# Numerators and denominators by tokens for the first four head pairs of an attention-and-MLP kernel, in a new order

## The chip, the cores and the metric

One NeuronCore of one Trainium2 chip runs the whole program. The metric is the device time of one execution in microseconds (us); lower is better. The engines are TensorE (PE in the profile, with its weight loads as PEld), VectorE (DVE), ScalarE (ACT), GpSimd (POOL) and SyncE (SP), whose queue issues the DMAs. Each works through its own list of instructions in the order in which it was written, and waits on the others through semaphores.

## What is computed

Attention with random features, then a two-layer MLP with SiLU. For 8 batches of 8 heads, 576 tokens, head size 64 and 128 features:

```python
def phi(x):                                  # x: [tokens, 64] of one head
    proj = x @ omega.T                       # 128 features
    h = proj - sum(x * x) / 2
    return exp(h - max(h)) / sqrt(128)       # the maximum over the features
q_p, k_p = phi(q * scale), phi(k * scale)
kv  = k_p.T @ v                              # 128 x 64
z   = sum of k_p over the tokens             # 128
num = q_p @ kv                               # tokens x 64
den = q_p @ z + 1e-6                         # one number a token
attn = num / den
x = attn with the 8 heads side by side       # 4608 x 512
out = silu(x @ w_in) @ w_out                 # 512 -> 2048 -> 512
```

## The kernel before

Two heads make a **pair**; there are 32 pairs (n = 0 to 31), four of them a tile of tokens (one batch). Tile t of the MLP needs the pairs 4t to 4t+3. The MLP of the first three tiles is done plainly, in 16 steps f a tile (`stage1`, L886, three fp32r matmuls of 512 columns for each of the four pairs; then `silu`, `g_low`, and `stage2`, L1132). The rest goes through a scheme with fewer products (L971, L1085), which the change does not touch.

What a pair takes, with the engine of each step:

- `project` and `project_mid` (PE, L541, L547): features of 9 chunks of 128 tokens, tokens on the partitions. Chunk 4 holds 64 tokens of either head.
- `square` (ACT, L524), `square_sum` (DVE, L533), `top` (DVE, L554 and L556), `shift` (DVE, L562): the bias of the exponential.
- `expo` (ACT, L579): the features `hk` and `hq`, 128 tokens x 128 features a chunk.
- `zsum_direct` (PE, L628, L630): ten matmuls with a block of ones stationary and the features of k moving give z, repeated on all partitions.
- `kv` (PE, L651): ten matmuls with V stationary (64 columns wide, the two heads side by side) and the features moving. They give kv with V's columns on the partitions, so `kt_copy` (ACT, L656), `kv_turn` (PE, L659) and `kw_copy` (ACT, L664) turn it.
- `denom` (DVE, L639): ten fused multiply-and-sums of `hq` with z, each followed by a read of the accumulator, then a reciprocal (L644).
- `normal` (POOL, L669): three multiplications of `hq` by the reciprocal.
- `turn` (PE, L675) and `en_copy` (ACT, L685): the divided features with the features on the partitions.
- `numer` (PE, L711): four matmuls, kv stationary, features moving, in two rows of 512 and two of 64 columns; they give x with its columns on the partitions.
- `x_high` (ACT, L730), `x_low` (DVE, L735), `x_rest` (ACT, L740): x in two parts, as `stage1` wants it.

From pair 8 on z is summed on POOL, and from pair 5 on kv of the next pair and the numerator are one step; neither is changed.

The MLP's weights come as 64-bit words. For each block, ACT makes a scaled copy (`exponent`, L795), DVE builds the 32-bit number in three steps (`word`, L809, L811, L815), and POOL splits it (`weight_high` L828, `weight_low` L832).

The order on every engine is made when the program is built. A planner (`Plan.run`) takes one step after another by a due time (`key`), with costs (`COST`) and a table of shifts (`SHIFTS`, two characters a step) that moves each due time. PSUM has eight banks in four pools (`acc` 4, `h` 1, `fx` 1, `att` 2), given in turn. Where the planner sees PE idle it puts in filler matmuls on `ones` (`pulses`, L500), whose result nobody reads.

Of the kernel before, what the change touches and what calls it, by code (L numbers as in the profile page):

```python
# [42 lines left out]
LEAD = 4  # L43
WARM = 7
# [10 lines left out]
for _f in range(16):  # L55
# [3 lines left out]
HOMES |= {("raw", 3, "k"): "w12", ("raw", 3, "q"): "w13", ("v", 2): "w14", ("v", 3): "w15"}  # L59
PLAIN = 3  # L60
# [19 lines left out]
STAY = 5.387  # L80
HANDOFF = {"PE": 0.053, "ACT": 0.034, "DVE": 0.034, "POOL": 0.075, "SP": 0.08}
CALM = 0.341
JOIN = 0.929
WAIT_PE = 0.279
WAIT_ACT = 0.228
WAIT_DVE = 0.243
WAIT_POOL = 0.0
HASTE = 2.036
# [3 lines left out]
EASE = 0.082  # L92
# [11 lines left out]
    "nb": (0.29, 0.37), "ssum": (0.66, 0.745), "den": (3.41, 3.49),  # L104
# [10 lines left out]
    "AIAINlAIAIAIAIAIAIAIAIAqAIAIAPAIAIBXAIIhAIFMDPAIDrAIXZAOAIL0AIAIAIAIlUAIbNL-AIGTAILlYXAIAIAIZ1ALAIqbAICcCAJ1AI"  # L115
    "AIPLmFqsM6jGj+A6RmAIAkgMAIAiIvAIK7PnEpEkDhAJAIAISDAICbDJy9AIMlcGAIAIaLBJAIAIAmCToUFCDeAIAIAaAIAIFBNAc2AIvVAIv8"
    "cyD--4G8BnBqAIDyN9AIBjAbCjCeGwPwf5M2oxAIAIAI1YAIAIfvKUAIlAAIyJTCANqqE3CjT6AIAI-48PgXUTA3AIqVgEM7GqqoEaB3OHiXS7"
    "A0B6AOAIAde6AIMF9gTqNTAIBxMBSKAIAI5NAIAIfUhwSMAISBxVAIBqSpAIP7AIBal4tsAbOfAPAIrZv2nxm8AgAIAIS5JyJ+AIFeAJAIteLB"
    "O4E5R1EpENAICLAILNAIAIJfDhAIBwAIGPs4AIJrs7yrxrMlRPAIFIAgYaA3b9hRbmIIn9jzkT6LkovJsF29D+WOEC5KlVJbgh6nAIAkl6PAm6"
    "mkVzphES3T8Pha5xQn+L-UyFew72pi5OPWk0reil7VtnJIflaampwvp00rwVNdu0MlbFQ3mXIpFWXVQqTVWAh2n5lGMadWEFuMErPdltG3I-qz"  # L120
    "Njj8aLV-cUZEz92d39AIqdihAIAIfIA9w9AIA-+20PI88lPhg1dZAyrHN6CW-4JYJLhIAIm2YbHATZSbP1FlHzrMAIxbqCh6AeNPYGeEDRZFsK"
    "V260v0dWO17cdxwGIh6FFERZ7SVN8-6Y+ErCUPAIur-QGICPkQ3mTLqTgNn8yB455fx-u11n3A1DsOJatjjs09nPLXPmgj-4AIC2mdVWPZh82-"
    "xjzpvQAIvTynbmnYgSb8YhfaHoRB4R65pj6NcQmkjEKCYxVofLgLq1btU4iNXeYUbbXSJFJgWWTlLFaBSxmGFLebN1OuZIEtDlEoa0R6i-7i8X"
    "3hOpGSMDyZpXM2Tt2ybo2CJVdtsitDXRPPBkGPTrRwHVFvwHAIXXwOR4F3y+UOXAYYzBCySXA8JyWgRRRcG18vHmCFsmEaF6nJZphVkR6lzX-4"
    "NKBJG-eBVcLHUuEoOBldPSBWtZzb0g7eQKEPHZ6HLceiwdsoG-POE8yii5DsH3AIi4AIAIAIbuJqV+kQAuREAqDOOgAeLKbgknqhwCvE+IQzhg"
    "QOAwZFpr4WUm4Hg0aGD8FNti6bi6VFH2IGqIBHoaVEjfNNOh6+eqbJ1V0x+y-B8x0Tic5hQoMac2zg1AU7ODIYwaZWAIDXXm3hj6mvuUh6spNS"
    "pWcNUNLINoKMH2PyAIoB5TmFKvKzLZLQmZ6HVZ3oEekZAIVReEz17ryW6Mbok-b5LnPNrhg1YcRsjX0UeId1CSAIvxn4vpiAUDFvO0BFAIC+B0"
    "FrFbTvUEECApKUuSksWBUrCHlOJ0FR4dPNUzKgPYPHCfoc44rkr3rYtAP-4rXPDiOMMNLMMSaSAIMTgZEUAuFSNZL8UuSVPVG3AIBSWsE-fjVh"
    "BLA4B+UdAIr-+sR6EaYvI9vtY8APCsFFlNAIdWcsGVG-QnFjLDKYAMAIAISWU-F8kTZHJBCbAoBYZmAMAIASjIwU4xpv21AIAOkWdvQxIWC-r+"
    "mgHBGdytuN-3u2eyDdd5k1zrkcW-DD3qeEc0tElRgu4Gk1zWCyAINfAIs+dc0haFbJAeVF-4JQAI4FpQfP13979ut0A6RbRnZC1Vlye5qjFGf9"  # L130
    "AI8YzTcrjAAILGdf+6VRSKvcidj+knAIfq7erfv62f4uAsnO5ANEbyURoXRHOtRfUiq1BZGGmw9zei4+3L0hzY8diOuwwEcZiMmIB4Dq0ccHqj"
    "ss1b5wwcFV8dnUj2mooJCjAIbQYw42tdhH-4wU7MzYp1e5Z4xVwj6jdf7Wm1lA7l11dICcv7-4zT4D8ju2S3bPd+l7mDVTGqeoiNJq-45K3C7T"
    "FBAIElVBZG4FbZVFmongYIIr5w-48p5M-4-4yyx+AgJok5R47nL1-4AIsb-4efBt9-uV-4m48vvzXGBrNGjykkiQSkeImwQemccx6h-JIBAIDx"
    "BAsjRQPQzqA30by+Dvgrt9-4jsfBgCgUNKGUCow0nsRzn6iX5qO5c81AHeIRy-VPmd-4Cwl2qXuUQigIcVZQ3FabtQAIccGmAIAVqz-47rAITa"
    "bSyXyp3oiNLxWWLfeRp45c5O+L9AnBahluAjNPWhWj92TJ4OCbSElVAIDLYVLEQG4ec0eHnpgjJWD+AJJGZgWgSgF4RLWPD5ZTc1n9jqApAeAI"
    "S5HZAIFLFGFV1JBoWPridVw3w4iddKSCG0HGKQLjd8l6-etrFJ5HBuAI2AvQAIwCDdOEMSlsAIGusDD-KfAuHoE-IKzjJHUZXRLgEjAIGaE6He"
    "B+GuAOAIhqBHZ8bWbVl-ncsrsHk9BWKcmsAIUYqDF3EdYlSqGKAIObKQKvU3Hz8huAwNAIAvdxDfg0B9iHZ+zpk7T72f035xfBMt7iUKgzzSWa"
    "ZMA9G-Btu0734O4c8s8x3efhPGLLHoAIauBzmGFJtp3ohNAIo7c+gstbrhUjTZfTQEAIDoAncbA3T5AxBzGQZ8zbaHafNAJwnNAIaFm6uST0Td"
    "FMxeMLZcXKTFZLaE2fQPQtZAvWAIAIl0KoEEt1M5FOAIo5sLKtZDso1IhLfTAIAIOiOAIvatJpZzN7JletnCaGzBInAIZkcHDQY7k8UmVaWVXa"
    "B3EvAIAuCWFGBQAIAIQ5AIAIAIAIAIYiLFJ7AID4AISdMzdRzchYXaWBAIjAmWI4AIHCdSAIMjzYxxc1vgX+AIJoDbf3YE-4KeKGNCqBJgIZFn"  # L140
    "MoD8FbDUAIBdUclghSfZAIHBeYmxTvAIewdgEdHjlH+LqE9y1CCwfdz7dawYkYllPnmSj2ct-30evUcQbcgDJqBcBLxIYsC7jgtSo1wAmxyQp-"
    "nKdWh1dAMnrtbiZ9POaR4xqeL5rF1qYDxe1gIqlso-n-KgV3hzi+ryhMykJer4kn2M3w2YnzKY1HjnkttjgSBlsCYG4G0iucl+sundoMwLnOes"
# [48 lines left out]
)  # L191
HOT = 100.0
PULSE = 0.24
IDLE = 0.791
PAD = 0.288
EARLY = 0.9

# [80 lines left out]
class Plan:  # L278
# [20 lines left out]
    def cost(self, u):  # L299
# [15 lines left out]
        if kind == "sums":  # L315
            return ((0.79, 0.83), (0.79, 0.83), (0.79, 0.83), (0.45, 0.49), (0.45, 0.49))[n[2]]
        if kind == "wd" and n[-1] == 0:
            return 0.34, 0.42
# [145 lines left out]
def attention_mlp(ctx: ExitStack, tc: tile.TileContext, qT, kT, qn, kn, v, om_in, w_in, w_out, out, out_t):  # L464
# [53 lines left out]
    def load_v(n):  # L518
        T["v", n] = vt = new(HOMES.get(("v", n), "v"), [P, NC + 1, D])
        nc.sync.dma_start(vt, v[divmod(n, NPAIR)])  # L520
# [1210 lines left out]
```

## Time and profile before

| | us |
|---|---|
| median of 3 runs | 1010.08 (1009.83 to 1011.92) |
| the profiled execution | 1008.95 |
| span of its instructions | 1007.2 |
| PE busy in the span | 982.9 (98%) |
| DVE busy | 758.1 (75%) |
| ACT busy | 637.4 (63%) |
| POOL busy | 394.2 (39%) |
| mean granted TensorE clock | 0.995 |

A matmul on fp32 data shows as two records, each with its weight load; records overlap, so what a matmul takes on PE is the distance from one start to the next, not the length of a record. A wait in brackets stands on the instruction that waited, with the one that ended it.

### The profile page before, as it was taken

The numbers are of one execution on the slowest core, as the hardware profiler recorded it, in microseconds if no ns is written. First come the engines' busy times: TensorE is split into PE (matmuls) and PEld (weight loads), VectorE is DVE, ScalarE is ACT, GpSimd is POOL, SyncE is SP. The second block draws the span as 40 slices with busy tenths as digits, with TensorE's granted clock in tenths as the row PEclk, the third lists the DMA queues.
The fourth block names the chain that finished last, engine by engine and source line by source line (L and its number), as shares of the span: only waits on it lengthen the run. The fifth ranks groups of instructions, "written<-read, shape, count | busy, mean of one in ns | idle before, by whom it ended". The sixth has DMA issues, their size and how long they took to land.

```text
span 1007.2 us, 17418 instructions
## 1 busy us (share of the span) xinstructions
PE 982.9 (98%) x5790; PEld 784.8 (78%) x5790; DVE 758.1 (75%) x1899; ACT 637.4 (63%) x1239; POOL 394.2 (39%) x495
## 2 busy tenths in 40 slices
PE   8789999999999999999999989999999999999998
PEld 7577777777777777778778768777878777888886
DVE  7997988776677767897667799994649987546953
ACT  7778574656557766658988756667678554334541
POOL 1544564677888777654555321330112010000000
PEclk9999999999999999999999999999999999999999
DMA  9757777777777886749788657876545677656682
GB/s 352 284 181 247 257 238 232 243 245 215 262 240 241 273 284 189 265 137 300 270 289 286 213 180 249 270 245 207 167 159 172 203 263 256 194 190 189 188 277 99
DMA packets 107593, 232.94 MB, mean 231 GB/s; under 512 B 14705, under 2 KB 39409, under 8 KB 107505
## 3 DMA queue, kind: packets, MB, share of 16 engines
q1 hardware_dynamic: 107344, 231.58, 70.0%
q8 instruction: 46, 0.75, 0.3%
q14 instruction: 43, 0.34, 0.1%
q10 hardware_dynamic: 160, 0.26, 0.1%
HBM read 182.52 MB, written 49.28 MB: 230 GB/s over the span
## 4 chain that ended last, share of the span: by engine, by line
PE 78%; DVE 15%; ACT 3%; DMA 2%; issue 1%; SPq 0%; DVEq 0%; ACTq 0%
PE ps_acc L971 17%; PE ps_acc L1132 12%; PE ps_acc L1085 11%; PE ps_h L886 7%; PE ps_fx L886 5%; PE ps_att L541 4%; PE ps_att L651 2%; DVE prod L639 2%; PE ps_att L1085 2%; PE ps_att L711 2%; DVE w L1075 2%; PE ps_fx L971 2%; PE ps_att L971 2%; PE ps_h L971 2%; PE ps_h L1085 2%; PE ps_fx L1085 2%
## 5 line engine op out<-in xcount | busy, mean ns | idle before, releaser
L971 PE MATMUL ps_acc<-w,x 128*128 128x512 f32 x768 | 185.8, 395 | 0.3 <-DVE wraw L1018 0.2
L971 PEld LDWEIGHTS ps_acc<-w,x 128*128 128x128 f32 x768 | 141.9, 188 | 32.7 <-DVE wraw L1018 0.8
L669 POOL TENSOR_TENSOR hq<-hq,rd 128x384 f32<-128x384 f32 x96 | 88.6, 947 | 187.8 <-DVE rd L644 144.2
L1132 PE MATMUL ps_acc<-wo,gh 128*128 128x512 f32 x384 | 123.3, 402 | 0.0
L1085 PE MATMUL ps_acc<-w,x 128*128 128x512 f32 x426 | 108.6, 397 | 0.1
L886 PE MATMUL ps_h<-x,w 128*128 128x512 f32 x360 | 97.2, 403 | 0.6 <-ACT gf L1025 0.3
L1085 PEld LDWEIGHTS ps_acc<-w,x 128*128 128x128 f32 x426 | 79.9, 190 | 18.0 <-DVE w L1075 0.6
L1132 PEld LDWEIGHTS ps_acc<-wo,gh 128*128 128x128 f32 x384 | 68.4, 188 | 14.4
L886 PEld LDWEIGHTS ps_h<-x,w 128*128 128x128 f32 x360 | 64.5, 188 | 15.2 <-ACT gf L1025 1.4
L1132 PE MATMUL ps_acc<-wo,gl 128*128 128x512 f32 x192 | 75.4, 393 | 0.4 <-DVE gl L1029 0.4
L1085 PE MATMUL ps_acc<-gh,x 128*128 128x512 f32 x196 | 70.0, 397 | 0.4 <-DVE gf L1105 0.4
L602 POOL TENSOR_TENSOR t<-hk 128x256 f32<-128x256 f32 x48 | 38.2, 816 | 57.5 <-ACT hk L579 31.4
L1029 DVE TENSOR_TENSOR gl<-gf,gh 128x512 fp32r<-128x512 f32 x48 | 44.4, 931 | 17.3 <-ACT gf L1025 17.1
L886 PE MATMUL ps_fx<-x,w 128*128 128x512 f32 x216 | 56.7, 399 | 0.0
L886 PEld LDWEIGHTS ps_fx<-x,w 128*128 128x128 f32 x216 | 39.4, 188 | 10.1 <-issue 1.1
L639 DVE CUSTOM_DVE_ANT_0 prod<-hq,ps_att 128x128 f32<-128x128 f32 (+1 forms) x140 | 40.1, 287 | 8.1 <-PE ps_att L622 2.5
L1085 PEld LDWEIGHTS ps_acc<-gh,x 128*128 128x128 f32 x196 | 36.8, 188 | 9.2 <-DVE gf L1105 0.8
L524 ACT ACTIVATE nat<-nat 128x576 f32<-128x576 f32 x58 | 40.1, 703 | 4.8 <-DMA nat<-qn 2.8
L1132 PEld LDWEIGHTS ps_acc<-wo,gl 128*128 128x128 f32 x192 | 36.0, 188 | 9.0 <-DVE gl L1029 1.0
L685 ACT COPY en<-ps_att 128x384 f32<-128x384 f32 x55 | 25.7, 480 | 22.5 <-PE ps_att L675 18.0
L608 POOL TENSOR_TENSOR t<-t,hk 64x128 f32<-64x128 f32 x48 | 25.0, 520 | 34.6 <-ACT hk L579 31.9
L1085 PE MATMUL ps_acc<-gl,x 128*128 128x512 f32 x98 | 38.3, 391 | 0.0
(464 smaller groups left out, 2461.4 us busy)
## 6 DMA issues: line engine op xcount, KB each, us to landing
x<-ws SPq DMA_DIRECT2D x84, 512.0 KB, 4.2
x<-wt SPq DMA_DIRECT2D x44, 512.0 KB, 4.0
wo<-wo_d SPq DMA_DIRECT2D x32, 512.0 KB, 4.8
x<-wo_d SPq DMA_DIRECT2D x64, 256.0 KB, 3.3
rawk<-kT SPq DMA_DIRECT2D x30, 352.0 KB, 3.9
rawq<-qT SPq DMA_DIRECT2D x30, 352.0 KB, 4.8
v<-v SPq DMA_DIRECT2D x30, 320.0 KB, 4.6
nat<-kn SPq DMA_DIRECT2D x29, 288.0 KB, 4.5
```

The source lines that it names most:

```text
L524: nc.scalar.activation(nat, nat, AF.Square, scale=SCALE * 0.5**0.5)
L541: nc.tensor.matmul(ps[:, i * M : (i + 1) * M], raw[r, o : o + P], oms[r], start=True, stop=True)
L602: nc.gpsimd.tensor_tensor(t[:, step], e[:, 5 * step : 5 * step + 2], e[:, 5 * step + 2 : 5 * step + 4], ALU.add)
L608: nc.gpsimd.tensor_tensor(es[r, j], es[r, j], e[r, MID], ALU.add)
L639: nc.vector.tensor_tensor_reduce(out=prod[r], in0=e[r, c], in1=z[r, j * M : (j + 1) * M], scale=1.0, scalar=GUARD, op0=ALU.mult, op1=ALU.a ...
L669: nc.gpsimd.tensor_tensor(e[:, c], e[:, c], rd[:, c].unsqueeze(2).broadcast_to([P, 3, M]), ALU.mult)
L685: nc.scalar.copy(T["en", n][:, 3 * g * P : 3 * (g + 1) * P], T.pop(("t", n, g)))
L886: nc.tensor.matmul(ph, w[:, i], x[:, j], start=k == 0 and n == 0, stop=k == NK - 1 and n == 2)
L971: nc.tensor.matmul(ph, ws[:, u, kk * P : (kk + 1) * P], o[:, x], start=i in (0, 1, 4) and kk == 0 and n == 0, stop=kk == 1 and n == 2, ski ...
L1029: nc.vector.tensor_tensor(gl, T.pop(("gf", t, f)), T["gh", t, f].bitcast(F32), ALU.subtract)
L1085: nc.tensor.matmul(T["qb", p, chain][d], w[:, u, d * P : (d + 1) * P], x, start=i in (0, 1, 4) and s == 0 and n == 0, stop=s == NS - 1 and ...
L1132: nc.tensor.matmul(T["po", t][j], g[:, js], w, start=f == 0 and n == 0, stop=f == NF - 1 and n == 2)
```

## The change

For the pairs 0 to 3 (`SHARE = 4`) the steps from z to x are replaced:

- `marks` (DVE) fills three blocks of 64 columns behind V with ones, and with zeros on the other head's half for chunk 4; `load_v` brings V in front of them. V of the four pairs has homes of its own, the later x buffers `x01` to `x31`.
- `kv_wide` (PE) has the features stationary and moves V's 64 columns and a block of 64 ones: kv and z come out together, features on the partitions. Nothing has to be turned. `kz_copy` (ACT) copies 65 columns a head.
- `turn` and `en_copy` take the features of q undivided.
- `numer_rows` (PE) has 128 tokens of the turned features stationary and moves the 65 columns: numerators and denominator by tokens, ten matmuls.
- `divide` (DVE) adds the guard, takes the reciprocal and multiplies: six instructions.
- `rows_turn` (PE) turns the result in five transposes, before `x_high`, `x_rest` and `x_low` as they were.

`zsum_direct`, `kv`, `kt_copy`, `kv_turn`, `kw_copy`, `denom` and `normal` are no longer run for these pairs. Constants of the planner and the whole table of shifts are new, so the order is new on every engine to the end of the program.

```diff
+SHARE = 4
+HOMES |= {("v", n): f"x{n}1" for n in range(4)}
-STAY = 5.387
+STAY = 9.083
-CALM = 0.341
-JOIN = 0.929
+CALM = 0.133
+JOIN = 7.97
-IDLE = 0.791
-PAD = 0.288
+IDLE = 1.237
+PAD = 1.63
 SHIFTS = (
...
 )
+    def marks(n):
+        T["v", n] = vt = new(HOMES["v", n], [P, NC + 4, D])
+        nc.vector.memset(vt[:, NC + 1 :], 1.0)
+        for j in range(2):
+            nc.vector.memset(vt[(1 - j) * D : (2 - j) * D, NC + 2 + j], 0.0)
...
+    def kv_wide(n, ps):
+        e, vt = T["h", n, "k"], T.pop(("v", n))
+        for j in range(2):
+            for i in range(5):
+                c, one = (i + 5 * j, NC + 1) if i < 4 else (MID, NC + 2 + j)
+                nc.tensor.matmul(
+                    ps[:, 2 * j * D : 2 * (j + 1) * D], e[:, c], vt[:, c + j : one + 1 : one - c - j], start=i == 0, stop=i == 4
+                )
+        T["kv", n] = ps
+
+    def kz_copy(n):
+        T["kw", n] = kw = new("kw", [P, 2, D + 1])
+        nc.scalar.copy(kw, T.pop(("kv", n))[:, : 4 * D].rearrange("p (j d) -> p j d", j=2)[:, :, : D + 1])
+
+    def numer_rows(n, a, b):
+        new_x(*divmod(n, NPAIR))
+        T["num", n] = a, b
+        for i in range(5):
+            ps, at, lo = (a, i, i * P) if i < 3 else (b, i - 3, min(i * P, S - P))
+            for j in range(2):
+                nc.tensor.matmul(
+                    ps[:, (2 * at + j) * (D + 1) : (2 * at + j + 1) * (D + 1)], T["en", n][:, j * S + lo : j * S + lo + P],
+                    T["kw", n][:, j], start=True, stop=True,
+                )
+
+    def divide(n):
+        T["xn", n], T["xo", n] = xn, xo = new("gf", [P, 4, P]), new("gl", [P, MAIN])
+        rd = xo[:, P : P + 10]
+        parts = [ps[:, : w * (D + 1)].rearrange("p (c d) -> p c d", d=D + 1) for ps, w in zip(T["num", n], (6, 4))]
+        for ps, lo, hi in zip(parts, (0, 6), (6, 10)):
+            nc.vector.tensor_scalar(rd[:, lo:hi], ps[:, :, D], GUARD, None, ALU.add)
+        nc.vector.reciprocal(rd, rd)
+        for ps, x, lo, hi in (
+            (parts[0], xn[:, :3].rearrange("p t d -> p (t d)"), 0, 6),
+            (parts[1][:, :2], xn[:, 3], 6, 8),
+            (parts[1][:, 2:], xo[:, :P], 8, 10),
+        ):
+            nc.vector.tensor_tensor(
+                x.rearrange("p (c d) -> p c d", d=D), ps[:, :, :D], rd[:, lo:hi].unsqueeze(2).broadcast_to([P, hi - lo, D]), ALU.mult
+            )
+
+    def rows_turn(n, c):
+        a, b = T["num", n]
+        xn, xo = T.pop(("xn", n)), T.pop(("xo", n))
+        for i in range(4):
+            nc.tensor.transpose(c[:, i * P : (i + 1) * P], xn[:, i], ident)
+        nc.tensor.transpose(b[:, 3 * P :], xo[:, :P], ident)
+        T["num", n] = [(c, 0, MAIN, 0), (b, MAIN, S, 3 * P + REST)]
```

**PE, from the end of pair 1's first projection to its second** (before): fillers, z of pair 0, kv of pair 0, fillers, the turn of kv.

```order
L547 MATMUL ps_att<-oms,rawk 128x128
L500 MATMUL ps_fx<-ones 128x128 x3
L628 MATMUL ps_fx<-hk,sides 128x128
L630 MATMUL ps_fx<-hk,ones 128x128 x4
L628 MATMUL ps_fx<-hk,sides 128x128
L630 MATMUL ps_fx<-hk,ones 128x128 x4
L651 MATMUL ps_att<-hk,v 64x128 x10
L500 MATMUL ps_att<-ones 128x128 x2
L659 MATMUL ps_att<-ident,kt 128x128
```

The same place after the change (`x_171` is V of pair 0 with its ones; L651 is now `kv_wide`, L737 `turn`, L666 `numer_rows`, L691 and L692 `rows_turn`). The second piece stands a dozen rows further on, at the numerators of the pairs 0 and 1.

```order
L554 MATMUL ps_acc<-oms,rawk 128x128
L554 MATMUL ps_h<-oms,rawk 128x128
L560 MATMUL ps_acc<-oms,rawk 128x128
L651 MATMUL ps_acc<-x_171,hk 128x128 x10
L737 MATMUL ps_acc<-ident,hq 128x128 x3
L554 MATMUL ps_fx<-oms,rawq 128x128
```

```order
L666 MATMUL ps_fx<-kw,en 128x65 x6
L666 MATMUL ps_acc<-kw,en 128x65 x4
L737 MATMUL ps_h<-ident,hq 128x128 x3
L737 MATMUL ps_att<-ident,hq 128x128 x6
L560 MATMUL ps_h<-oms,w_226 128x128
L666 MATMUL ps_att<-kw,en 128x65 x10
L691 MATMUL ps_fx<-ident,gf 128x128 x4
L692 MATMUL ps_acc<-ident,gl 128x128
```

z and kv are one run of ten matmuls, the turn of kv and the fillers are gone from here, and the turn of x comes one pair's numerator later than that x.

**DVE, the end of the first tile.** Before: the reciprocal that ends `denom` of pair 4, which follows that of pair 3, and the low part of pair 3 (`x_1035`) behind it.

```order
L644 RECIPROCAL rd<-den 128x9
L556 TENSOR_REDUCE smk<-ps_att 128x4
L556 TENSOR_REDUCE smk<-ps_acc 128x4
L562 TENSOR_REDUCE smk<-smk 128x2x4
L562 TENSOR_REDUCE nbk<-smk 128x2x4
L735 TENSOR_TENSOR x_1035<-ps_att,x_1035 128x512
```

After: `x_801` and `x_953` are the x of pairs 2 and 3, L676 to L683 are `divide` of pair 3, and the reciprocal on top ends `denom` of pair 4.

```order
L706 RECIPROCAL rd<-den 128x9
L797 TENSOR_TENSOR x_801<-ps_fx,x_801 128x512
L676 TENSOR_SCALAR gl<-ps_acc 128x6
L676 TENSOR_SCALAR gl<-ps_acc 128x4
L677 RECIPROCAL gl<-gl 128x10
L683 TENSOR_TENSOR gf<-ps_acc,gl 128x384
L683 TENSOR_TENSOR gf<-ps_acc,gl 128x128
L683 TENSOR_TENSOR gl<-ps_acc,gl 128x128
```

The low part of pair 2 and the division of pair 3 stand behind the denominators of pair 4, which is not one of the changed pairs.

**SP, the first loads.** Before:

```order
L512 DMA rawk<-kT 128x704
L516 DMA nat<-kn 128x576
L512 DMA rawq<-qT 128x704
L516 DMA nat<-qn 128x576
L512 DMA rawk<-kT 128x704
L520 DMA v<-v 128x640
```

After:

```order
L518 DMA rawq<-qT 128x704
L522 DMA nat<-kn 128x576
L522 DMA nat<-qn 128x576
L518 DMA rawk<-kT 128x704
L522 DMA w_203<-kn 128x576
L522 DMA w_205<-qn 128x576
```

The input of pair 0's projection of q comes first and that of k fourth. The input of pair 1's k, the fifth row before, now stands behind both natural loads of pair 1 and two loads of V.

## Rows read from the trace of the kernel before

**Rows 1.** Page, part 2: PE's busy tenths in 40 slices of 25.2 us.
```profile
PE   8789999999999999999999989999999999999998
```

**Rows 2.** Windows: length; busy PE, PEld, DVE, ACT, POOL; PE's clock; DMA.
```profile
0.00:80.65 80.65, 68.97 (x579) 55.51 (x579) 68.62 (x219) 58.50 (x166) 31.72 (x42) 0.96 0.76 270
...
80.65:1007.20 926.55, 913.90 (x5213) 729.27 (x5211) 689.50 (x1681) 578.90 (x1074) 362.46 (x454) 1.00 0.70 228
```

**Rows 3.** Waits in the first 81 us: engine, line, whom for, us, times, longest.
```profile
PE ps_acc L675 <- POOL hq L669: 3.4, 6, 1.1
```

**Rows 4.** Windows around the slow stretch, columns as in rows 2.
```profile
44.00:48.00 4.00, 1.99 (x12) 1.61 (x12) 3.86 (x13) 1.75 (x7) 2.40 (x3) 0.92 0.65 253
48.00:54.00 6.00, 5.80 (x39) 4.78 (x39) 5.83 (x13) 5.40 (x17) 2.07 (x2) 0.50 0.62 197
```

**Rows 5.** Timeline of PE: start, us, line, records.
```profile
10.95 0.39 PE L628 MATMUL ps_fx<-hk,sides 128*128 128x128 f32 x2
...
13.28 1.31 PE L651 MATMUL ps_att<-hk,v 128*64 128x128 f32 x20
...
22.19 0.55 PE L675 MATMUL ps_fx<-ident,hq 128*128 128x128 f32 x3
...
24.91 1.19 PE L711 MATMUL ps_acc<-en,kw 128*64 128x512 f32 x8
26.07 0.33 PE L659 MATMUL ps_h<-ident,kt 128*128 128x128 f32 x1
27.95 2.05 PE L500 MATMUL ps_h<-ones 128*128 128x128 f32 x16 [1.55 <-ACT kw L664]
29.75 1.26 PE L886 MATMUL ps_h<-x,w 128*128 128x512 f32 x3
...
54.79 0.28 PE L711 MATMUL ps_fx<-en,kw 128*64 128x64 f32 x4
55.00 0.49 PE L547 MATMUL ps_att<-oms,w 128*128 128x128 f32 x2
```

**Rows 6.** Timeline of DVE: its first wait, one `denom` from end to end, `x_low`.
```profile
5.73 0.75 DVE L533 TENSOR_REDUCE smk<-nat 128x9 f32<-128x576 f32 x1 [4.45 <-ACT nat L524]
...
25.74 0.28 DVE L639 CUSTOM_DVE_ANT_0 prod<-hq,ps_att 128x128 f32<-128x128 f32 x1
...
29.58 0.64 DVE L735 TENSOR_TENSOR x<-ps_acc,x 128x512 fp32r<-128x512 f32 x1
30.14 0.74 DVE L533 TENSOR_REDUCE smq<-w 128x9 f32<-128x576 f32 x1
30.80 0.74 DVE L533 TENSOR_REDUCE smq<-nat 128x9 f32<-128x576 f32 x1
31.46 0.28 DVE L554 TENSOR_REDUCE smk<-ps_fx 128x1 f32<-128x128 f32 x1
31.77 0.17 DVE L562 TENSOR_REDUCE smk<-smk 128x9 f32<-128x18 f32 x1
...
32.07 0.76 DVE L809 TENSOR_SCALAR w<-wraw 128x512 uint32<-128x512 uint32 x2
...
18.69 1.23 DVE L556 TENSOR_REDUCE smq<-ps_acc 128x4 f32<-128x512 f32 x2
```

**Rows 7.** Timelines of DVE and POOL where both read SBUF; DVE's last row here is `g_low`.
```profile
49.05 0.69 DVE L811 SCALAR_TENSOR_TENSOR w<-wre,w 128x512 uint32<-128x512 uint32 x1
...
51.93 1.76 DVE L811 SCALAR_TENSOR_TENSOR w<-wre,w 128x512 uint32<-128x512 uint32 x1
...
76.47 1.61 DVE L1029 TENSOR_TENSOR gl<-gf,gh 128x512 fp32r<-128x512 f32 x1
...
51.81 1.33 POOL L832 TENSOR_TENSOR w<-w,w 128x512 fp32r<-128x512 f32 x1
...
29.81 2.40 POOL L669 TENSOR_TENSOR hq<-hq,rd 128x384 f32<-128x384 f32 x3 [2.57 <-DVE rd L644]
```

**Rows 8.** Timeline of PE, the longest wait behind the first 81 us.
```profile
604.13 0.87 PE L675 MATMUL ps_fx<-ident,hq 128*128 128x128 f32 x3 [3.54 <-ACT hq L579]
```

## What the change was predicted to do

> **What bounds the kernel now.** I read the page's slices first, then windows, then the waits, then the timelines. PE is full from the fourth slice to the end; only the first three slices are at 7 and 8 tenths [rows 1]. So the time is the work of PE plus what PE loses, and what the change can win lies in the first 80 us. There PE is busy 68.97 of the 80.65 us before the first matmul of the second layer, so 11.7 us are idle; in all the rest it is idle 12.7 of 926.6 us [rows 2]. Two more losses hide in the busy share. The planner put in 16 filler matmuls: eight of them fill 1.80 us from 27.95 to 29.75 [rows 5], so 16 are 3.6 us. And the granted clock is 0.50 from 48 to 54 us, the lower level, behind a stretch in which PE was busy for half the time [rows 4]; 5.8 us of work at half speed are 2.9 us lost. So 80.65 us hold 69.0 - 3.6 - 2.9 = 62.5 us of work at full speed, and 18 us of loss.
>
> DVE is the other busy engine there, 68.6 of 80.65 us [rows 2]. What PE waits for longest by sum is POOL's division of the features (3.4 us), and its fillers at 27.95 waited 1.55 us for the copy of the turned kv [rows 3, 5]; both stand on the chain denominators, division, turn, numerator that the change rebuilds.
>
> **The change part by part.**
>
> *DVE.* One `denom` holds the engine from 25.74 to the next instruction at 29.58, 3.84 us [rows 6]; four go, -15.4. `divide` isn't in the trace. Its three products have 384, 128 and 128 columns; `x_low` takes 0.56 for 512 (29.58 to 30.14) and the one-chunk maximum 0.31 for 128 (31.46 to 31.77) [rows 6]. By columns that is 0.42 + 0.2 to 0.31 twice, and three tiny instructions at about 0.2 each (the shift's takes 0.17). Floor 1.1, ceiling 1.9; I take 1.4, as the products are throughput work like `x_low`: +5.6. The twelve memsets fall into DVE's first wait of 4.45 us [rows 6] and cost nothing; were that hole gone, some 2 us. Sum on DVE: -9.8 us.
>
> *PE.* Removed for each pair: z, 10.95 to 13.28, 2.33; kv, 1.31 with its tail, some 1.2; the numerator, 24.91 to 26.07, 1.16; the turn of kv, 0.2 to 0.3 of its 0.33 [rows 5]. That is 4.95. Added: `kv_wide`, the same shapes as z, 2.33; five turns, where three take 0.55 with their tail [rows 5], some 0.65; `numer_rows`. Ten of its matmuls have a 128-wide stationary and move 65 columns, which no row shows. Floor: two matmuls of a 64-wide stationary and 64 columns take 0.21 (54.79 to 55.00) [rows 5], so ten 1.05 if only the moving counted. Ceiling: ten of z's shape, 2.33. I take 2.3: in that pair the two heads lie side by side and would stream together, so its 0.21 looks like two weight loads one behind the other, and this step loads twice as wide. So +5.3 - 4.95 = +0.3 a pair, +1.3 in all; with the floor -3.6.
>
> (The Trainium skill, TensorE: Matmul & The Clock Gate, section LDWEIGHTS, says that a weight load costs by its columns, 107 ns for 128, which speaks against having the tokens stationary. Two loads a matmul make 2.1 us, as I take; its streaming rule alone would make the sum 4 us better.)
>
> *POOL.* Three multiplications a pair go, 2.40 us [rows 7], 9.6 in all, and with them PE's 3.4 us of waits except those of pair 4. Do they free DVE as well? DVE slows where POOL reads SBUF and DVE does too: one step of the weights takes 1.76 instead of 0.69 while POOL splits one, `g_low` 1.61 [rows 7]. But beside a division (29.81 to 32.2) [rows 7] DVE's sums take 0.74, their usual [rows 6]: I count nothing. `divide` has one operand in PSUM, as the maxima have that run beside POOL unslowed, so I add nothing for it either.
>
> *ACT.* One copy of kv less and one of 130 columns instead of 128: nothing.
>
> *Order.* I went through the new order by hand with durations of rows. Ahead of the first `g_low`, DVE now has 16 natural sums (0.66), 24 maxima of a bank (two take 1.23), 11 of a chunk (0.31), 14 pairs of shifts (0.30) [rows 6], 23 steps of weights (some 0.57), four divisions, four low parts and pair 4's `denom`: 58 us. Before, the same count is 68 us (two maxima fewer, three steps of weights more, five `denom`); from 5.73 that would end at 74, and it ends at 78.1 [rows 6, 7], 4 us of waits and collisions. With the same 4 us the new one ends at about 68.
>
> **The sum.** PE must do, up to its first matmul of the second layer, 62.5 + 1.3, three fillers (0.7), and 0.2 more of other work (nine first-layer matmuls fewer, pair 4's numerator and pair 5's kv more): 64.7 us. It can't begin the second layer before DVE's 68, so that is the floor. With all of the old idle time and the old slow stretch it would be 64.7 + 11.7 + 2.9 = 79.3. The truth lies between, since several waits are taken away and a new one comes: `stage1` of pair 2 needs `x_low`, which now stands behind the 3.8 us of pair 4's `denom` on DVE, and pair 3's numerator, one chunk and one projection are all that PE has meanwhile. I take the middle, 73.5. Then PE is 80.65 - 73.5 = 7.2 us earlier, with 0.2 more done: **7.3 us**. Behind it PE is full, so it keeps them: DVE's work left there is the same. The new table moves the rest too; I count nothing for it, with 4 us either way, since one single wait there is 3.54 us [rows 8]. The profiled execution, 1008.95 with a span of 1007.2, becomes 1001.6; the median of the runs, 1.1 us above it, becomes 1002.8.
>
> **The rivals.**
>
> *A. Given back in the first tile.* PE enters the MLP earlier and waits there for weights, which DVE, ACT and POOL still have to build; of 7.3 us some 4 come back as idle time between 75 and 150 us. For it: DVE is the engine whose queue decides even now. Against: DVE gains more (9.8) than PE. Time: 1006.8.
>
> *B. The later order is better as well.* The wait of 3.54 us at 604 us and the slow matmul behind it (0.87 for three turns) [rows 8] don't come again: 4 to 5 us more. For it: the table is new from end to end, and that wait hangs on one exponential that came late. Against: such a wait can come elsewhere. Time: 998.5.
>
> *C. Slower: the clock.* Only 3 of 16 fillers are left. Where PE is busy for half the time, the clock goes to its lower level for 6 us, and 2.9 us are lost [rows 4]. If the new thin places (the first 13 us, the wait for pair 2) and the two first tiles bring four such stretches instead of one, that is 8.7 us more, and with new waits of 1 us the time is 1012.5. It decides from three stretches more on. For it: the fillers that kept the clock are gone. Against: the old 16 did not prevent the one at 48 us, and PE has more real work to put in the gaps.
>
> *D. Nothing is gained.* The removed work was not what PE waited for: DVE is relieved, but the loads and the chain of exponentials set the pace, and PE's idle time stays (79.3): 1.5 us gained, 1008.6. Against: the waits for POOL and the turned kv are in the rows.
>
> **How the numbers follow.** Forecast (7.3 us, from 4 to 10) 0.48; A 0.14; B 0.17; C 0.10; D 0.11. The range: from B's 998 with a little to spare to D's upper side, 1009.5; left out are C and the tails of B. About 0.2% (2 us) is what a measurement of this kernel can tell from no change. Faster: the forecast, B and A (3.3 us), less a part of A: 0.77. Within: D and that part: 0.14. Slower: most of C: 0.09.
>
> **What would show it.** Right: the first matmul of the second layer near 73.5 us, DVE's first `g_low` ending near 70; `numer_rows` at 2.2 to 2.4 us a pair, `divide` near 1.4; POOL without work until the first weights. Wrong: that matmul beyond 78; granted clock at 0.50 in more than 6 us of the first 80; idle time of PE between 75 and 150 us above 6 us; or a difference that comes from behind 200 us.

## The result, and the profile after

| | before | after |
|---|---|---|
| median of the runs taken together, us | 1010.61 (1009.83 to 1011.92) | 997.73 (997.24 to 999.52) |
| profiled execution, us | 1008.95 | 997.93 |
| its span, us | 1007.2 | 996.1 |
| first matmul of the second layer at, us | 80.65 | 71.75 |
| from there to the end, us | 926.55 | 924.35 |

The changed kernel is faster: the ratio of the times is 0.9874, with a 95% interval of 0.9857 to 0.9892. Predicted were 1002.8 us, and a range of 997.5 to 1009.5. Between the profiled executions the gain is 11.0 us; of the 11.1 between their spans, 8.9 lie in the stretch up to the first matmul of the second layer and 2.2 behind it.

The slices of PE from the page of the changed kernel, to be held against [rows 1]: the slices of 7 and 8 tenths behind the first are gone.

```profile
PE   8999999999999999999999989999999999999998
```

Windows of the changed kernel, columns as in [rows 2] (length; busy PE, PEld, DVE, ACT, POOL; granted clock; share and GB/s of DMA). The second starts at 16 us, behind PE's last wait for a load; the third is the 100 us behind the stretch:

```profile
0.00:71.75 71.75, 64.60 (x557) 56.45 (x558) 59.93 (x170) 57.16 (x165) 18.14 (x27) 0.95 0.82 296
16.00:71.75 55.75, 51.99 (x472) 45.02 (x472) 50.06 (x139) 49.11 (x145) 16.84 (x18) 1.00 0.81 290
71.75:171.75 100.00, 100.00 (x594) 80.53 (x593) 88.71 (x207) 74.30 (x138) 56.93 (x55) 1.00 0.75 256
71.75:996.10 924.35, 913.55 (x5193) 729.97 (x5191) 684.29 (x1682) 577.51 (x1068) 362.46 (x457) 1.00 0.70 229
```

In the first stretch PE's idle time falls from 11.7 us [rows 2] to 71.75 - 64.60 = 7.15, that is by 4.5, and its busy time by 4.4; 13 fillers that are gone account for 2.9 of that (0.225 us each by [rows 5]). DVE's busy time falls by 8.7, its idle time hardly moves (12.0 to 11.8). The third row rules out that the gain was given back in the first tile. From 16 us on PE is idle for 55.75 - 51.99 = 3.76 us, where the kernel before was for 10.05; its waits for POOL's division [rows 3] and for the turned kv [rows 5] are gone. The longest that is left there (columns as in [rows 3]):

```profile
PE ps_h L948 <- DVE x L797: 0.6, 1, 0.6
```

The new steps on PE, from its timeline (start, us, line, records): `kv_wide` is L651, `numer_rows` L666, the turns of x L691 and L692, `stage1` L948; the row at 8.16 is the projection of k of pair 0, the last one the first of the second layer.

```profile
8.16 2.08 PE L554 MATMUL ps_acc<-oms,rawk 64*128 64x128 f32 x16 [2.02 <-DMA rawk<-kT]
...
14.55 2.44 PE L651 MATMUL ps_acc<-x,hk 128*128 128x128 f32 x20
16.84 0.49 PE L737 MATMUL ps_acc<-ident,hq 128*128 128x128 f32 x3
...
26.91 2.45 PE L666 MATMUL ps_att<-kw,en 128*128 128x65 f32 x20
29.19 0.60 PE L691 MATMUL ps_fx<-ident,gf 128*128 128x128 f32 x4
29.84 0.37 PE L554 MATMUL ps_acc<-oms,w 64*128 64x128 f32 x1
...
57.74 2.34 PE L666 MATMUL ps_acc<-kw,en 128*128 128x65 f32 x20
...
61.38 0.96 PE L948 MATMUL ps_h<-x,w 128*128 128x512 f32 x3
...
65.19 0.72 PE L948 MATMUL ps_h<-x,w 128*128 128x512 f32 x2 [0.62 <-DVE x L797]
...
71.75 0.62 PE L1194 MATMUL ps_acc<-wo,gh 128*128 128x512 f32 x2
```

By the starts, `kv_wide` takes 2.29 us and `numer_rows` 2.28 here, 2.17 to 2.18 in the other three pairs. From DVE's timeline one `divide`, the start of pair 4's `denom` (L701) and `x_low` of pair 2 behind it (L797), and the first `g_low` (L1091):

```profile
26.73 0.15 DVE L676 TENSOR_SCALAR gl<-ps_fx 128x6 f32<-128x6 f32 x1
...
27.24 0.56 DVE L683 TENSOR_TENSOR gf<-ps_fx,gl 128x384 f32<-128x384 f32 x1
...
28.11 0.28 DVE L567 TENSOR_REDUCE smk<-ps_h 128x1 f32<-128x128 f32 x1
...
57.43 0.28 DVE L701 CUSTOM_DVE_ANT_0 prod<-hq,ps_acc 128x128 f32<-128x128 f32 x1
...
60.84 0.63 DVE L797 TENSOR_TENSOR x<-ps_fx,x 128x512 fp32r<-128x512 f32 x1
...
68.83 0.69 DVE L1091 TENSOR_TENSOR gl<-gf,gh 128x512 fp32r<-128x512 f32 x1
```

A division takes 28.11 - 26.73 = 1.38 us. `g_low` ends at 69.52, and at 71.75 PE goes from `stage1` into the second layer without a wait. The granted clock of 0.50 has moved from 48 to 54 us [rows 4] to 8 to 14 us, as these windows show (columns as above):

```profile
6.00:8.00 2.00, 0.14 (x2) 0.00 (x0) 0.82 (x2) 1.37 (x2) 0.00 (x0) 0.84 0.95 365
8.00:14.00 6.00, 5.84 (x40) 5.35 (x40) 5.48 (x13) 3.09 (x9) 0.00 (x0) 0.50 1.04 415
```

Ahead of it PE is idle for 2.02 us, waiting for k of pair 0. Behind the first stretch the longest wait is now 1.5 us instead of the 3.54 of [rows 8]:

```profile
581.50 1.31 PE L713 MATMUL ps_fx<-hk,v 128*64 128x128 f32 x20 [1.52 <-ACT hq L592]
```

### The profile page after: what moved, and what is told of

It is laid out like the page before. It is cut to its first block, busy times and chain, and to the rows that moved or that the text cites. A ratio compares the mean times of both kernels' runs of the same rounds, so it can differ in the third digit from the quotient of the medians.

```text
span 996.1 us, 17264 instructions
## 1 busy us (share of the span) xinstructions
PE 978.1 (98%) x5748; PEld 786.4 (79%) x5748; DVE 744.2 (75%) x1851; ACT 634.7 (64%) x1231; POOL 380.6 (38%) x483
## 4 chain that ended last, share of the span: by engine, by line
PE 80%; DVE 10%; ACT 4%; POOL 3%; DMA 2%; issue 2%; SPq 0%; POOLq 0%; DVEq 0%; ACTq 0%
PE ps_acc L1033 19%; PE ps_acc L1147 15%; PE ps_acc L1194 11%; PE ps_h L948 7%; PE ps_fx L948 4%; PE ps_att L554 3%; PE ps_att L1147 3%; PE ps_att L1033 2%; PE ps_att L713 2%; PE ps_h L1147 2%; DVE prod L701 1%; PE ps_att L773 1%; PE ps_att L737 1%; PE ps_h L1033 1%; PE ps_fx L1147 1%
## 5 line engine op out<-in xcount | busy, mean ns | idle before, releaser
L1033 PE MATMUL ps_acc<-w,x 128*128 128x512 f32 x816 | 197.8, 396 | 0.0
L1033 PEld LDWEIGHTS ps_acc<-w,x 128*128 128x128 f32 x816 | 150.5, 188 | 33.9 <-DVE w L1080 0.3
L731 POOL TENSOR_TENSOR hq<-hq,rd 128x384 f32<-128x384 f32 x84 | 75.4, 922 | 167.1 <-DVE rd L706 166.9
L1147 PE MATMUL ps_acc<-w,x 128*128 128x512 f32 x426 | 107.7, 395 | 0.2 <-DVE w L1137 0.2
L948 PE MATMUL ps_h<-x,w 128*128 128x512 f32 x384 | 102.7, 402 | 1.6 <-POOL w L894 0.6
L1147 PEld LDWEIGHTS ps_acc<-w,x 128*128 128x128 f32 x426 | 79.4, 188 | 18.8 <-DVE w L1137 0.9
L948 PEld LDWEIGHTS ps_h<-x,w 128*128 128x128 f32 x384 | 68.8, 188 | 18.2 <-POOL w L894 1.1
L1194 PEld LDWEIGHTS ps_acc<-wo,gh 128*128 128x128 f32 x384 | 68.6, 188 | 14.2
L701 DVE CUSTOM_DVE_ANT_0 prod<-hq,ps_att 128x128 f32<-128x128 f32 (+1 forms) x170 | 48.8, 287 | 14.4 <-PE ps_att L635 8.6
L1091 DVE TENSOR_TENSOR gl<-gf,gh 128x512 fp32r<-128x512 f32 x48 | 42.5, 888 | 16.0 <-ACT gf L1087 16.0
L948 PE MATMUL ps_fx<-x,w 128*128 128x512 f32 x192 | 49.4, 398 | 0.0
L537 ACT ACTIVATE nat<-nat 128x576 f32<-128x576 f32 x58 | 39.9, 695 | 4.8 <-DMA nat<-kn 3.4
L948 PEld LDWEIGHTS ps_fx<-x,w 128*128 128x128 f32 x192 | 35.2, 188 | 7.8 <-issue 0.2
L569 DVE TENSOR_REDUCE smq<-ps_att 128x4 f32<-128x512 f32 x44 | 29.0, 683 | 9.9 <-PE ps_att L554 9.4
```

Source lines behind the costliest of these rows:

```text
L537: nc.scalar.activation(nat, nat, AF.Square, scale=SCALE * 0.5**0.5)
L569: nc.vector.tensor_reduce(m[:, 5 * j : 5 * j + 4], ps.rearrange("p (c m) -> p c m", m=M), AX.X, ALU.max)
L701: nc.vector.tensor_tensor_reduce(out=prod[r], in0=e[r, c], in1=z[r, j * M : (j + 1) * M], scale=1.0, scalar=GUARD, op0=ALU.mult, op1=ALU.a ...
L731: nc.gpsimd.tensor_tensor(e[:, c], e[:, c], rd[:, c].unsqueeze(2).broadcast_to([P, 3, M]), ALU.mult)
L948: nc.tensor.matmul(ph, w[:, i], x[:, j], start=k == 0 and n == 0, stop=k == NK - 1 and n == 2)
L1033: nc.tensor.matmul(ph, ws[:, u, kk * P : (kk + 1) * P], o[:, x], start=i in (0, 1, 4) and kk == 0 and n == 0, stop=kk == 1 and n == 2, ski ...
```

## The experiments

The theory was the prediction's: DVE sets the end of the first stretch, the new steps take some 10 us off it, and the 2 us behind come from the new table. Its rivals: the table gave it all; POOL's relief and the port gave it; PE's own chain gave it. The ratio behind each time is to the kernel before, run on the same chip.

### Steps and tables exchanged

The first run takes the shifts of before for all units but those of pairs 0 to 3, and the constants of before, such as:

```
-STAY = 9.083
+STAY = 5.387
...
-JOIN = 7.97
+JOIN = 0.929
```

> The new steps of the four pairs stay, and so does the place of these pairs' own units; every other unit gets the shift that it had before, and the planner gets its constants of before. Theory (the steps, by the vector engine's relief, gave the first stretch; the new table gave only the 2 us behind it): the first matmul of a second layer near 72 to 75 us, the program at 999 to 1004 us, and waits of TensorE of the size seen before somewhere behind the first stretch. Rival (the table gave most of the 13 us, and the steps would gain little without it): first second-layer matmul near 77 to 80 us, program at 1006 to 1011 us.

The second takes the steps of before with the constants and, by the units' names, the shifts of the changed kernel:

```
-SHARE = 4
+SHARE = 0
```

> The four pairs take the steps of before (numerator by features, denominator by its own sums on the vector engine); constants and shifts are those of the changed kernel, by the units' names. Theory (the steps gave the first stretch): first second-layer matmul at 79 to 82 us, program at 1006 to 1011 us, that is at most 3 us faster than before, by what the table alone gives later. Rival (the table gave most): first second-layer matmul at 73 to 76 us, program at 999 to 1003 us.

Measured: 1045.51 us (1.0354, 1.0332 to 1.0377) and 1049.32 (1.0392, 1.0371 to 1.0413). Both theories missed both runs by some 35 us. The first second-layer matmul came at 85.22 and 84.26, and the rest was longer too. PE's longest waits of the first kernel, over the whole span (engine, line, whom for, us, times, longest), and its window behind the first stretch:

```profile
PE ps_acc L1147 <- DVE w L1137: 6.1, 4, 3.3
PE ps_att L635 <- ACT hk L592: 3.7, 1, 3.7
```

```profile
85.22:1044.80 959.58, 919.72 (x5163) 728.95 (x5161) 679.03 (x1672) 572.59 (x1061) 355.72 (x453) 0.99 0.66 219
```

PE is idle 39.9 us there, against 10.8 in the changed kernel. The likely reason, which no run isolates, is that the shifts suit one set of steps and are just wrong numbers with others. So the exchange says that a wrong order costs some 36 and 40 us over the kernel before, three times the change, and it can't say which part of the 11 us is the steps'. That needs runs that leave an order alone and change the work in it.

### The old order, relieved

In `denom` of the kernel before, fewer sums:

```
+        if n < 4:
+            nc.vector.memset(den, 1.0)
-        for c in range(NC):
+        for c in range(3 if n < 4 else NC):
```

> The kernel before, its order and steps untouched, but in the first four pairs 7 of the 10 sums of each denominator are left out (a memset fills their columns), so the output of these pairs is not the reference's. The vector engine loses 7 * 0.37 us - 0.1 us = 2.5 us a pair, 10 us in all, the saving that the change brought. Theory (the vector engine's load sets the first stretch in either order): first matmul of a second layer at 71 to 74.5 us instead of 80.65, program at 1000 to 1004 us. Rival (the relief is worth its time only in the order that was fitted to it; in the old order other engines' places hold the stretch): first second-layer matmul at 77 to 80.5 us, program at 1006.5 to 1010 us.

And with that, POOL's products left out:

```
     def normal(n, g):
+        if n < 4:
+            return
```

> The kernel before in its order; in the first four pairs 7 of the 10 sums of each denominator are left out as in the run with fewer sums, and GpSimd's three products of normalization per pair too (2.4 us a pair and the wait of TensorE for them), so the output of these pairs is not the reference's. With fewer sums alone the first second-layer matmul came at 77.44 instead of 80.65 us. Theory A (what still held the old order was the chain over GpSimd, 1.6 us of waits of the turns for it and what follows from them): first second-layer matmul at 72 to 75 us, program at 1001 to 1005 us. Theory B (the places in the old order, fitted to the old durations, hold it whatever is relieved, through many short waits): 76 to 77.5 us, program at 1005.5 to 1008 us.

Measured: 1007.61 us (0.9979, 0.9966 to 0.9992), and with POOL relieved as well 1008.14 (0.9983, 0.9970 to 0.9997). The first second-layer matmul came at 77.44 and 77.66, against 80.65. So the theory fell for the old order: some 10 us less on DVE brought 3.2 us there, as the rival had it, and POOL's work nothing more (theory B, just above its bounds). Windows from 16 us to that matmul: the kernel before, the run with fewer sums, the run with both.

```profile
16.00:80.65 64.65, 54.60 (x458) 42.71 (x458) 58.76 (x193) 48.27 (x138) 30.42 (x33) 0.95 0.73 258
```

```profile
16.00:77.44 61.44, 50.71 (x459) 40.43 (x458) 51.80 (x142) 47.97 (x139) 30.39 (x33) 1.00 0.76 270
```

```profile
16.00:77.66 61.66, 50.59 (x459) 40.37 (x458) 51.79 (x142) 48.11 (x139) 20.86 (x21) 1.00 0.77 270
```

Before, DVE is busy for 91% of its window and PE for 84%. Relieved, DVE is busy for 84% and PE for 83%: neither is full, and PE waits in many short pieces for ACT, DVE and POOL. The longest, in the run with both:

```profile
PE ps_h L500 <- ACT kw L666: 2.1, 1, 2.1
```

The granted clock was whole in both runs, which may be up to 2.9 of the 3.2 us. Of these 3.2, two were lost again behind the stretch (928.56 us instead of 926.55 with fewer sums). That is rival D, in the old order. (The Trainium skill, Perfetto Trace Analysis, section Identifying the Most-Contended Engine, has the engine with the highest occupancy optimized first, TensorE judged by other measures, its weight loads among them; here that was DVE with 91%, beside 66% of PEld, and taking 10 us off it alone was worth 3.)

The 3.5 us wait of [rows 8] was there again in both; this row is from the timeline of the run with fewer sums:

```profile
602.33 0.87 PE L677 MATMUL ps_fx<-ident,hq 128*128 128x128 f32 x3 [3.51 <-ACT hq L579]
```

It belongs to the old order: every kernel with the changed kernel's steps and order had a longest wait of 1.5 us behind the first stretch, but for the one below without norms (0.8).

### DVE in the new order: more work, and less

At the end of `divide`, seven dead sums, and in a second run three:

```
+        spare = new("den", [P, NC])
+        for c in range(7):
+            nc.vector.tensor_tensor_reduce(
+                out=prod, in0=ident, in1=T["num", n][0][:, :M], scale=1.0, scalar=GUARD, op0=ALU.mult,
+                op1=ALU.add, accum_out=spare[:, c : c + 1],
+            )
```

> Seven dead fused multiply-and-sum instructions of about 0.33 us stand at the end of each of the four divisions, about 2.3 us a pair on the vector engine, 9.2 us in all, near what the change took off it; TensorE, ScalarE and GpSimd have the work of the changed kernel. Theory (the vector engine's load sets the first stretch): first second-layer matmul 6 to 9 us later than the changed kernel's 71.75, program at 1003 to 1007 us. Rival (the relief of GpSimd and of the shared port, or the shorter chain of TensorE, gave it): first second-layer matmul within 2.5 us of 71.75, program under 1000.5 us.

> As the run with the vector engine's work put back, with three dead sums a pair instead of seven: some 1.1 us a pair, 4.4 us in all. Seven put the first second-layer matmul 8.7 us later (about 3 us of it a stretch of half clock at 30 to 38 us that the change has not), while 14 us less work brought 0.65 us. Theory A (the changed kernel stands at the point where the vector engine begins to bind, so added work counts nearly in full and relief nothing): 3.5 to 5.5 us later than 71.75, program at 1000.5 to 1004 us. Theory B (it has some 3 us of slack there): 0.5 to 2.5 us later, program at 998 to 1000.5 us.

In `square_sum` and `shift`, the sums of norms left out:

```
-        nc.vector.tensor_reduce(T["sm", n, who][:, 1, :NC], T.pop(("nat", n, who)), AX.X, ALU.add, negate=True)
+        nat = T.pop(("nat", n, who))
+        if n >= 8:
+            nc.vector.tensor_reduce(T["sm", n, who][:, 1, :NC], nat, AX.X, ALU.add, negate=True)
...
+        if n < 8:
+            nc.vector.tensor_scalar(part(T["nb", n, who]), part(sm[:, 0]), -1.0, None, ALU.mult)
+            return
```

> The changed kernel; in pairs 0 to 7 the vector engine's 16 sums over the squared features are left out (0.745 us each), and the two small sums of the shift become one negation (0.17 us less each): the squared norm stands in both the exponent and its maximum, so the result keeps its value. ScalarE still squares, the loads stay. Some 14 us less on the vector engine up to 71.75 us, whose busy time there is 59.93 us. Theory (with the vector engine's load gone TensorE is the next bound, whose work up to there was 64.6 us busy, some 2.9 us of it from the half clock at 8 to 14 us): first second-layer matmul at 65 to 68.5 us, program at 990 to 994.5 us. Rival (ScalarE or the loads of the start hold the stretch as much as the vector engine does, so a further relief is worth little): first second-layer matmul at 70 us or later, program above 995.5 us.

Measured: seven sums back, 1009.68 us (1.0007, 0.9991 to 1.0023); three, 1003.91 (0.9950, 0.9932 to 0.9967); the sums of norms left out, 997.68 (0.9872, 0.9849 to 0.9894). The first second-layer matmul came at 80.45, 76.05 and 71.10 us. Windows from 16 us to that matmul, seven sums, three sums, and no norms' sums:

```profile
16.00:80.45 64.45, 55.52 (x475) 47.75 (x473) 58.22 (x196) 49.54 (x146) 16.96 (x18) 0.95 0.71 250
```

```profile
16.00:76.05 60.05, 53.81 (x471) 46.29 (x470) 54.52 (x166) 49.50 (x145) 18.46 (x19) 0.97 0.79 273
```

```profile
16.00:71.10 55.10, 52.56 (x480) 46.13 (x479) 43.37 (x117) 49.01 (x144) 17.20 (x19) 1.00 0.82 295
```

DVE is busy for 90, 91 and 79% of these, and for 90% in the changed kernel and 91% in the one before. Work put back counts nearly in full: 28 sums of 0.33 us are 9.2 us and cost 8.7; twelve are 4.0 and cost 4.3. A third or more of that came over the clock, which fell to 0.50 behind longer waits of PE for DVE (1.07 and 1.49 us), where the changed kernel has it whole; here the run with seven sums and that with three:

```profile
31.42:38.25 6.83, 5.82 (x31) 5.30 (x32) 6.55 (x27) 4.13 (x13) 0.00 (x0) 0.50 0.29 95
```

```profile
68.45:71.86 3.41, 3.41 (x25) 2.67 (x26) 3.41 (x7) 2.26 (x3) 1.88 (x2) 0.50 0.67 224
```

PE's work at half speed there is up to 2.9 and 1.7 us of the two costs; 5.8 and 2.6 are left for the sums themselves. By the medians the two runs are 12.0 and 6.2 us behind the changed kernel, more than the work put back, of which 2.4 and 0.8 lie behind the stretch; the time of the first was 2.7 us above what the theory gave. Work taken off, some 10 us there, brought 0.65, so there the rival held. PE, busy for 95%, is then the nearest bound. Of the two theories on three sums, A holds: the changed kernel stands at the point from which DVE binds, with PE just beside it.

### POOL

In `rows_turn`, so behind the division and not ahead of it:

```
+        spare = xo[:, 2 * P :].rearrange("p (c m) -> p c m", m=M)
+        for _ in range(4):
+            nc.gpsimd.tensor_tensor(
+                spare, ident.unsqueeze(1).broadcast_to([P, 2, M]), ones[:, :2].unsqueeze(2).broadcast_to([P, 2, M]), ALU.mult
+            )
```

> Four dead multiplications of 256 columns on GpSimd stand ahead of the division of each of the four pairs, some 2.2 us a pair, near what the change took off GpSimd. Theory (GpSimd's relief is worth nothing, since it waits for the vector engine's parts of the weights): the program within 1 us of the changed kernel's 997.7. Rival (its instructions slow the vector engine's that run beside them, as in the row of 1.76 us for 0.69, and this was part of the gain): 2 to 4 us slower, 999.5 to 1002 us.

Measured: 998.61 us (0.9880, 0.9862 to 0.9898), first second-layer matmul at 72.22. POOL was busy 10.7 us longer up to there (28.89 instead of 18.14), DVE 0.7. As the theory has it: POOL's work beside DVE's is worth 0.5 us in the stretch and 0.9 between the medians, and the intervals of the two kernels overlap. Nothing waits for these products, so the run does not put back the waits of PE for POOL's division; in the old order, leaving the division out gave nothing more.

### The half clock at the start, and the loads behind it

Nine fillers ahead of the projection of k of pair 0, where the units are emitted:

```
+            if u["name"] == ("proj", 0, "k"):
+                pulses(ps[0], 9)
```

> Nine matmuls into a bank that is overwritten later are put ahead of the projection of k of pair 0, into the 2.02 us in which TensorE waits for a load at 6.1 to 8.2 us, behind which it was granted 0.50 of its clock up to 14.1 us. If TensorE's own time decides the first stretch from its start, the clock stays at 1.0 and the 2.9 us that the half clock cost come back: first second-layer matmul near 69 to 70 us, program 2 to 3 us under the changed kernel (994.5 to 996). If the vector and scalar engines, which fall behind later in the stretch, set its end, the half clock lay under their cover: the granted clock is whole, and the program ends within 0.7 us of the changed kernel (997.7).

And, without fillers, two loads moved ahead of others:

```
+        for name, ahead in ((("raw", 0, "k"), ("nat", 0, "k")), (("raw", 1, "k"), ("nat", 1, "k"))):
+            names = [u["name"] for u in units]
+            units.insert(names.index(ahead), units.pop(names.index(name)))
```

> The changed kernel with two loads moved ahead on their queue: k of pair 0 and of pair 1 for the projections before the token-major k and q of the same pair; all work stays. Theory (TensorE's 2.02 us wait for k of pair 0 and the half clock behind it cost little, since the sums of norms that now come later are waited for instead, as the fillers showed): program within 1 us of the changed kernel's 997.7. Rival (the order of the loads is what the start is bound by): first second-layer matmul 1.5 to 3 us earlier than 71.75, program at 994.5 to 996.5 us.

Measured: fillers, 998.25 us (0.9893, 0.9873 to 0.9913), first second-layer matmul at 72.12; loads moved, 1000.73 (0.9908, 0.9889 to 0.9927), at 73.13. PE's timeline with the fillers (L506, 18 records from 6.46 on):

```profile
6.46 2.17 PE L506 MATMUL ps_acc<-ones 128*128 128x128 f32 x18
8.70 1.16 PE L554 MATMUL ps_acc<-oms,rawk 64*128 64x128 f32 x16
...
12.76 0.37 PE L554 MATMUL ps_acc<-oms,rawk 64*128 64x128 f32 x1 [1.81 <-DMA rawk<-kT]
```

The clock stayed whole, the projection took 1.16 us instead of 2.08, and then PE waited 1.81 us for the next load, k of pair 1. So most of the half clock at 8 to 14 us lay under the loads, which run at 415 GB/s in that time. Not all of it need have: the run of the last experiment below has the changed kernel's own code up to its end, and in its profile the clock stayed whole without fillers.

```profile
8.00 1.16 PE L554 MATMUL ps_acc<-oms,rawk 64*128 64x128 f32 x16 [1.54 <-DMA rawk<-kT]
...
12.03 0.37 PE L554 MATMUL ps_acc<-oms,rawk 64*128 64x128 f32 x1 [1.78 <-DMA rawk<-kT]
...
70.46 0.62 PE L1194 MATMUL ps_acc<-wo,gh 128*128 128x512 f32 x2
```

It waits for the same load, but comes to the second layer at 70.46, 1.3 us earlier. So the half clock may have cost up to 1.3 of its 2.9 us, and the same code differs by 1.3 us there between two profiles: the 0.65 us of the run without norms' sums and the 0.5 of POOL's are within that.

With both k loads moved ahead, DVE had no sums of norms to shift by, and a bank came free late; PE's row:

```profile
13.99 0.80 PE L560 MATMUL ps_acc<-oms,rawk 128*128 128x128 f32 x2 [3.89 <-ACT hk L592]
```

That is 3 us slower than the changed kernel, where one theory had at most 1 us and the other a gain: loads moved ahead hold up loads that are waited for as well.

### The norms left out altogether

For all pairs, `square_sum` and `shift` as in the run without sums, and in `load_nat` and `square`:

```
-        nc.sync.dma_start(nat, (kn if who == "k" else qn)[divmod(n, NPAIR)])
...
-        nc.scalar.activation(nat, nat, AF.Square, scale=SCALE * 0.5**0.5)
```

> The changed kernel without the squared norms of all pairs: no loads in their token-major form, no squares on ScalarE, no sums on the vector engine, and one negation for the shift's two small sums; the norm stands in both the exponent and its maximum and cancels, so the result keeps its value. Up to 16 us the loads of the start fall by a third. With the vector engine's sums alone left out the first second-layer matmul came at 71.10 us, TensorE busy 52.56 of the 55.10 us from 16 us on. Theory (both TensorE from 16 us on and the loads ahead of it bind): the loads of k come 1.5 to 3 us earlier, the half clock at 8 to 14 us does not come, first second-layer matmul at 66 to 69.5 us, program at 991.5 to 996 us. Rival (the first stretch is bound by TensorE's list alone and the planned order keeps the other waits): above 70 us, program at 996.5 to 998 us. Behind the first stretch TensorE is busy 97 to 100% of nearly every window, so neither expects more than 2 us there.

Measured: 992.11 us (0.9826, 0.9808 to 0.9845), 5.6 us under the changed kernel and the best of all; the two intervals do not overlap. Windows up to the first second-layer matmul and behind it:

```profile
16.00:69.75 53.75, 51.05 (x465) 44.35 (x463) 44.41 (x114) 40.66 (x126) 16.83 (x19) 0.99 0.60 202
```

```profile
69.75:991.40 921.65, 912.55 (x5193) 729.99 (x5191) 646.79 (x1527) 551.22 (x1021) 366.73 (x456) 1.00 0.65 215
```

The first matmul at 69.75 us is just outside what the theory gave (66 to 69.5): 2.0 us of the gain are there, and 2.7 behind it, more than either theory had and not explained by any run. In the expectation the half clock was to stay away; it came once more, at 14 to 17 us. The result keeps its value: the squared norm stands in the exponent and in its maximum, so it need not be computed at all.

### What `numer_rows` is bound by

```
+        for wide, cols in ((128, 128), (128, 65), (128, 33), (64, 128), (64, 65), (64, 33)):
+            for _ in range(16):
+                nc.tensor.matmul(ps[:wide, :cols], ones[:, :wide], ident[:, :cols], start=True, stop=True)
```

> The changed kernel with 96 dead matmuls behind its end, 16 each with a stationary of 128 columns and 128, 65 and 33 moving columns, and of 64 columns with the same three; all float32. The time of the whole grows by theirs, only their rows matter. Theory (numerator by rows is bound by its weight loads: 2.17 to 2.28 us for ten matmuls of 65 moving columns): some 0.21 to 0.23 us each with 128 stationary columns, whatever moves, and about half of it with 64 columns and 65 or fewer moving. Rival (it is bound by what moves, and ten matmuls took 2.2 us for their waits): the time falls with the moving columns from 128 to 65 to 33 at 128 stationary columns, to 0.12 us or less at 65.

Measured: the groups of these matmuls by shape; "128*64" is a stationary of 64 columns, "128x65" 65 moving ones, and a float32 matmul leaves two records, so that x32 are 16.

```profile
L1754 PE MATMUL ps_acc<-ident,ones 128*128 128x128 f32 x32 | 3.7, 275 | 0.0
L1754 PE MATMUL ps_acc<-ident,ones 128*128 128x33 f32 x32 | 3.7, 276 | 0.0
L1754 PE MATMUL ps_acc<-ident,ones 128*64 128x128 f32 x32 | 3.7, 274 | 0.0
L1754 PE MATMUL ps_acc<-ident,ones 128*128 128x65 f32 x32 | 3.7, 273 | 0.0
L1754 PE MATMUL ps_acc<-ident,ones 128*64 128x65 f32 x32 | 2.0, 222 | 0.0
L1754 PE MATMUL ps_acc<-ident,ones 128*64 128x33 f32 x32 | 2.0, 222 | 0.0
```

With 128 columns stationary 16 matmuls take 3.7 us, 0.23 each, whether 128, 65 or 33 columns move; with 64 stationary 0.125, unless 128 move. With 128 columns stationary it is thus the load, or what goes with it, that sets the time, and not what moves; that is the case of `numer_rows`. What bounds the rows of 0.125 the runs don't tell. Ten matmuls are 2.3 us, the ceiling that the prediction took. (The Trainium skill, TensorE: Matmul & The Clock Gate, section LDWEIGHTS, gives a load's time as its columns divided by 1.2, in ns, so 107 for 128; 3.7 us over 32 loads are 116.)

## Why the prediction was right, and where its reasons were not

**The terms of the sum.** `divide` was taken at 1.4 us: 1.38. `numer_rows` at 2.3, near the ceiling: 2.17 to 2.28. POOL's work and the port at nothing: under 1 us, by the run with POOL's work put back. The first `g_low` was to end near 70 us: 69.5. All of that stands.

**The first stretch, 73.5 us.** It was the middle between DVE's floor of 68 and a ceiling of 79.3, and came at 71.75; so the term of 7.3 us measured 9.1 (8.9, and 0.2 more done). In it, 64.7 us were PE's work at full speed and 8.8 its loss. Measured are 64.60 - 2.9 = 61.7 us of work, and 7.15 of idle time with 2.9 of half clock, 10.1 of loss. So what was mis-sized is PE's work, 3.0 us too much, while the loss was 1.3 larger than taken; that the middle came so near is in part luck. Of the 3.0, some 0.6 are the new steps (5.1 us a pair by the starts, not 5.28), and 0.76 the first projection of the program, which took 1.85 us before (4.77 to 6.62) and 1.09 after (4.56 to 5.65). The rest is open. The wait that was to keep PE from the floor, `stage1` of pair 2 for `x_low` behind pair 4's `denom`, did not come. DVE had `denom` done at 60.84, 3.4 us after its start, and PE's numerator of pair 3, one chunk and one projection lasted from 57.74 to 61.38. The 0.62 us at 65.19 are for `x_low` of pair 3.

**The reason for it.** I argued that DVE's queue decides even in the kernel before, so that what comes off DVE comes off the time. Half of that held. In the new order work on DVE does count, upward: 9.2 us put back bring the stretch to 80.45, where it was before, a third of it over the clock. But in the old order 10 us less brought 3.2 us, up to 2.9 of them by the clock. The failing step is the one that read DVE's 68.6 of 80.65 us as the bound of the old order. There the places on the other engines were chosen with the longer DVE list in view, and that they held the stretch, through many short waits, is what is left when DVE's sums and POOL's products are out; no run shows it directly. Neither the relief in the old order nor either half of the exchange gave the 8.9 us; the steps with the order planned for them did. Which share the shorter chain on PE has (numerator and denominator in one, no turn of kv, no wait for the division ahead of the turns) stays open: the exchange of tables was to tell it and could not.

**Behind the first stretch.** Counted at 0 with 4 us either way, it was 2.0, the 2.2 less the 0.2 of work done earlier: PE's idle time there fell from 12.65 us to 10.80. Of these 1.85 us, 1.35 lie in the first 119 us behind the stretch (2.38 us idle before, 1.03 after), for which no run has the cause, and 0.5 in all the rest. Rival B had named the wait at 604 us; it shrank by 2.0, but 1.5 us of wait came elsewhere, so its price of 4 to 5 us was too high. The runs in the old order have that wait, those in the new don't, and the steps of the pairs there are the same in both, so this part is the order's.

**The rivals.** A did not happen (PE is busy 100.00 of 100 us behind the stretch). C happened once, as before, and not four times: 2.9 us of half clock, of which perhaps 1.3 came through. D is right for the old order alone. One of the signs of being wrong was touched all the same: the clock was at 0.50 for some 6.8 us and not 6 at most (0.84 of full already from 6 to 8 us, and 0.91 from 14 to 15). In the kernel before it was as long.

**The rest of the difference.** From 1002.8 to 997.7 are 5.1 us: 1.75 in the first stretch, 2.0 behind it, and 1.3 because the profiled execution of before lay 1.1 us under its median and that of after 0.2 above.

## What to carry to other kernels

A busy share of 90% does not say what a saving on that engine is worth. Leave the work out in the old order and see: if little comes, try the saving together with a new order, and don't expect the new order's own worth with the old work (36 and 40 us were lost by the exchange). Once a stretch is planned tight, put work back and take work off: here one direction cost its full price, a third of it over the clock, and the other brought less than two profiles of the same code differ by. So another bound stands beside DVE, and the next gain, 2.0 us in this stretch, came when loads and squares were relieved along with it.
